# Row numbers by the slot, a halved weight load doubled by ScalarE, and a last group in two pairs

## The chip, the cores and the metric

The kernel runs on one core of a Trainium2 chip. The core has five engines with a queue of instructions each, worked off in order: TensorE (PE; its weight loads are listed as PEld), VectorE (DVE), ScalarE (ACT), GpSimd (POOL) and SyncE (SP). In this kernel SP only issues plain transfers and POOL only issues gathers; both kinds run on the core's 16 DMA engines. The metric is the device time of one execution in microseconds; of several runs the median is given.

## The reference

The input x has 2048 tokens of 576 numbers. Two branches are computed and mixed by a gate per token:

```
g = sigmoid((x * gate_w).sum(-1))
a = irfft2(rfft2(x) * (w_r + 1j * w_i))
q1, q2 = halves of x @ w_q            # 32 heads, 128 numbers each
i1 = argmax(q1 @ k1.T); i2 = argmax(q2 @ k2.T)       # of 64 each
e = i1 * 64 + i2                      # one row of 4096, per token and head
b = sum over heads of  weight * gelu(x . u[e]) * v[e]
out = g * a + (1 - g) * b
```

The weight is a softmax over one candidate. u and v have 4096 rows of 576 numbers each.

## The kernel before

**Tiles.** The tokens are 16 tiles `t` of 128 tokens, one token to a partition. The 32 heads are 8 chunks `c` of 4. u and v lie side by side in one table `uv`, so that one gathered row of 1152 numbers brings both.

**Scores.** For each chunk `build_m` multiplies w_q with the keys, in five pieces of 128 of the 576 input columns (the fifth has 64 columns). `load_wq` brings each piece as 8 x 128 columns; in the fifth the 64 columns stand twice in memory, since the low and the high half of the bits of x are later multiplied with them in one go. A build needs its piece and is a run of 16 records on PE. `scores` then takes two tiles at a time, called a slot: PE makes 2 x 512 scores, DVE takes the maximum of each set of 64 (L419), ACT marks which scores are below it (the flags, L427) and adds offsets (L438), and DVE finds the first position by minima (L443, L447, L448, L450) and joins the two positions (L453). ACT writes the row numbers as integers into `ei` (L454). From L447 on this is done for two slots, that is four tiles, at once.

**Groups.** `group(t, c)` is the work of one tile and one chunk. POOL issues four gathers (L486), one a head; DVE makes four dot products with x (L495, whose sum is read out by a short second instruction), ACT takes gelu (L499), DVE multiplies with the weights (L500). Then either DVE adds the four rows of v, scaled, to the tile's sum `y` (L511 for the first, L513), or, for the tiles that `is_d` names, ACT makes four diagonal matrices (L523) and PE adds the rows up in PSUM; its result is taken over by ACT (L537) or DVE (L539). Tiles 0 to 9 have their groups among the scores of the chunks and after them. Tiles 10 to 15 have theirs at the end, in pairs (10, 11), (12, 13), (14, 15), chunk after chunk, so that the last two groups are those of tiles 14 (by PE) and 15 (by DVE) with chunk 7.

**Spectral branch.** When all scores are done, their memory is given to the Fourier branch: `fold`, `unit`, `invert`. `invert(t)` leaves a tile's share in `ga` (L825, L826). `mix` forms y = y * (1 - g) + ga on DVE (L830) and sends the tile out (L831).

**The order.** Every step is a job of a planner (`Plan.order`) before the program is built. A job has an engine, a duration that the planner assumes, a due time `at`, and the jobs and buffers that it needs. At each moment each engine takes, of the jobs that are ready in the planner's own account, the one that is due first; a due time is no earliest time. The planner assumes for a transfer 0.8 us after its issue, a time by its bytes, behind all the transfers before it, and 0.8 us more; for a gather that time is 1.55 us (L202 to L204, L235, L490), and 1.3 us for a change of ACT's table. The order that comes out is fixed for each engine's queue; on the chip a queue waits in that order for whatever is late. Loads and gathered rows share the 12 buffers `uv`; PSUM has four.

The due times that matter below: a load of wq is due 12 us before its slot; in the last group the dot products and sums are due at the group's time, tile 14's mix 2.4 us after it (9 after its own group, and groups are 6.6 apart), and tile 15's mix 9 us after it.

Of the kernel before, what the change touches and what calls it, by code (L numbers as in the profile page):

```python
# [225 lines left out]
def act(n):  # L226
    return 0.165 + n / 1200
# [8 lines left out]


@with_exitstack
def tile_kernel(ctx, tc, xn, xT, x5, wqT, kT, wri, uv, gw, t_kr, t_fi, t_tw, t_io, out):
    nc = tc.nc  # L240
    PS = bass.MemoryType.PSUM

# [71 lines left out]
    def ld(us, at, fn, w, r=(), **kw):  # L314
        return plan("SP", 0.06, at, lambda: on("SP", fn()), w, r, move=us, **kw)
# [22 lines left out]

    def load_wq(c, i, at, after=()):
        w = wq_t[c, i] = buf("uv", ROW, view=lambda x: x.rearrange("p a d -> p (a d)")[:, : 8 * P].rearrange("p (g e) -> p g e", g=8))  # L340
        ld(load(P * 4096, 4096), at, lambda: nc.sync.dma_start(w.ap, wqT[c, i]), [w], after=after)

    def load_x(b, i, at, at2, n=1):
        st = buf("uv", ROW, view=lambda x: x.rearrange("p a d -> p (a d)")[:, : n * 512])
# [49 lines left out]
    def scores(c, tp, at):  # L394
        if tp == 0:
            mx[c] = buf("mx", [P, NT, 2 * HPC])
        ps = psum()

        def part(j, i):
            t = 2 * tp + j  # L400
            b = t // 4
            tsl = slice((t % 4) * P, (t % 4) * P + P)
            mh, ml = m_t[c, i]
            x = xts[i if i < 4 else 8][b]
            seq = [(x, mh), (x, ml)] + ([(xts[4 + i][b], mh)] if i < 4 else [])

            def go():
                for n, (xx, m) in enumerate(seq):
                    mm(ps.ap[:, j, :], xx.ap[:, tsl], m.ap, start=i == n == 0, stop=i == 4 and n == len(seq) - 1)

            use = {id(q): q for pair in seq for q in pair}
            return plan("PE", 0.23 * len(seq), at, go, [(ps, j)], list(use.values()))

        seq = [(j, i) for i in range(ND) for j in range(2)] if tp in (0, 7) else [(j, i) for j in range(2) for i in range(ND)]
        js = [part(j, i) for j, i in seq]
        score_jobs[c, tp] = js
        mv = mx[c]
        s = c * 8 + tp
        dv(dve(1024, True), at, lambda: nc.vector.tensor_reduce(  # L419
            mv.ap[:, 2 * tp : 2 * tp + 2, :], ps.ap.rearrange("p a (g e) -> p a g e", e=E), AX.X, ALU.max),  # L420
            [(mv, tp)], [(ps, 0), (ps, 1)])
        sg = buf("sg", [P, 2, 2 * HPC, E], BF16)

        def signs(j, g0):
            def go():
                for g in range(g0, g0 + 4):
                    on("ACT", actv(  # L427
                        sg.ap[:, j, g, :], ps.ap[:, j, g * E : g * E + E], AF.Sign,
                        bias=mv.ap[:, 2 * tp + j, g : g + 1], scale=-1.0))
            plan("ACT", 4 * 0.216, at, go, [sg], [(ps, j), (mv, tp)])  # L430

        for j in range(2):
            for g0 in (0, 4):
                signs(j, g0)
        s2 = lambda: sg.ap.rearrange("p a g e -> p (a g) e")
        Q = E // 4
        for b in range(1, 4):
            ac(act(256), at, lambda b=b: actv(s2()[:, :, b * Q : b * Q + Q], s2()[:, :, b * Q : b * Q + Q], AF.Copy, bias=b / 4), [sg], [])  # L438
        if tp % 2 == 0:
            halves[:] = [buf("sq", [P, 2, 4 * HPC, E // 2], BF16)]  # L440
        sq = halves[0]
        k = tp % 2
        dv(0.07 + 512 / 1920, at, lambda: vt(sq.ap[:, k], s2()[:, :, : E // 2], s2()[:, :, E // 2 :], ALU.min), [(sq, k)], [sg])  # L443
        if k == 0:
            return
        q2 = lambda: sq.ap.rearrange("p s g e -> p (s g) e")
        dv(0.07 + 512 / 1920, at, lambda: vt(q2()[:, :, :Q], q2()[:, :, :Q], q2()[:, :, Q:], ALU.min), [sq], [(sq, 0), (sq, 1)])  # L447
        dv(0.07 + 512 / 1920, at, lambda: vt(q2()[:, :, :Q], q2()[:, :, :Q], ramp.ap[:, :Q].unsqueeze(1).to_broadcast([P, 8 * HPC, Q]), ALU.add), [sq], [ramp])  # L448
        im = buf("im", [P, 4, HPC, 2])
        dv(0.06 + 512 / 960, at, lambda: nc.vector.tensor_reduce(  # L450
            im.ap.rearrange("p a h b -> p (a h b)"), q2()[:, :, :Q], AX.X, ALU.min), [im], [sq])
        fe = buf("fe", [P, 4, HPC])
        dv(0.1, at, lambda: stt(fe.ap, im.ap[:, :, :, 0], float(E), im.ap[:, :, :, 1], op0=ALU.mult, op1=ALU.add), [fe], [im])  # L453
        ac(0.18, at, lambda: actv(ei[tp // 2][:, :, 4 * c : 4 * c + 4], fe.ap, AF.Copy, scale=float(E)), [("ei", tp // 2, c)], [fe])  # L454

    def soften(c, t0, t1, at):
        n = t1 - t0
# [18 lines left out]
    accs = {}  # L476
    sums = {}

    def group(t, c, at, ahead, gate_by=()):
        rows = []  # L480
        for k in range(HPC):
            g = buf(("uv", "uv2"), ROW)
            h = c * HPC + k

            def go(g=g, h=h):
                on("POOL", nc.gpsimd.indirect_dma_start(  # L486
                    out=g.ap.rearrange("p a d -> p (a d)"), out_offset=None, in_=uv,
                    in_offset=bass.IndirectOffsetOnAxis(ap=ei[t // 4][:, t % 4, h : h + 1], axis=0)))

            plan("POOL", 1.13, at - ahead, go, [(g, 0), (g, 1)], [("ei", t // 4, c)], move=1.55, after=gate_by)  # L490
            rows.append(g)
        z, b, a = (buf(n, [P, HPC]) for n in ("z", "b", "a"))
        x = xs[t]
        for k in range(HPC):
            dv(0.68, at, lambda k=k, g=rows[k]: stt(  # L495
                g.ap[:, 0, :], g.ap[:, 0, :], 1.0, x.ap, op0=ALU.mult, op1=ALU.mult, accum_out=z.ap[:, k : k + 1]),
                [(z, k), (rows[k], 0)], [x])
        zk = [(z, k) for k in range(HPC)]
        ac(0.18, at - 9, lambda: actv(b.ap, z.ap, AF.Gelu_apprx_tanh), [b], zk, table="gelu")  # L499
        dv(0.08, at, lambda: stt(a.ap, b.ap, 1.0, sw[:, t, c * HPC : c * HPC + HPC], op0=ALU.mult, op1=ALU.mult),  # L500
           [a], [b, ("sw", t, c)])
        new = t not in accs
        if not is_d(t, c):
            if new:
                accs[t] = buf("xn", [P, D])
            y = accs[t]
            for k in range(HPC):
                v = lambda k=k: rows[k].ap[:, 1, :]
                s = lambda k=k: a.ap[:, k : k + 1]
                if new and k == 0:  # L510
                    dv(0.4, at, lambda: nc.vector.tensor_scalar(y.ap, v(0), s(0), None, op0=ALU.mult), [y], [(rows[0], 1), a])  # L511
                else:
                    dv(0.73, at, lambda v=v, s=s: stt(y.ap, v(), s(), y.ap, op0=ALU.mult, op1=ALU.add), [y], [(rows[k], 1), a])  # L513
            return
# [61 lines left out]
    for s in range(NCH * 8):  # L576
# [18 lines left out]
            add_best(c, L0, NT, at + 6, lambda c=c: lc[:, :, c * HPC : c * HPC + HPC], ("lc", c))  # L595
        while todo and todo[0][0] * 8 / NE + LE <= s + 1:
            n, (t, cc) = todo[0]
            if cc * 8 + t // 4 * 2 + 1 > s or (t >= 8 and cc * 8 + 7 > s):
                break
            todo.pop(0)  # L600
            group(t, cc, due(n), AHEAD)
# [226 lines left out]
    def mix(t, at):  # L828
        ga, y = gas[t], accs[t]
        dv(0.73, at, lambda: stt(y.ap, y.ap, gone[:, t : t + 1], ga.ap, op0=ALU.mult, op1=ALU.add), [y], [(ga, 0), (ga, 1), "gone"])  # L830
        ld(load(P * 2304, 2304), at - 5, lambda: nc.sync.dma_start(out[t], y.ap), [], [y])  # L831

    TR = T0 + TLAG
# [9 lines left out]
    for n, t in enumerate(E_T + L_SEQ):  # L843
        at = inv0 + FPACE * 4.2 * n
        invert(t, at)
        if t in E_T:
            mix(t, at + 5)
    for n, (t, c) in enumerate(SEQ):
        group(t, c, TR + TGS * n, AHEAD, score_jobs[NCH - 1, 7][:1])
        if c == NCH - 1:  # L850
            mix(t, TR + TGS * n + 9)
    opened = False
    for j in plan.order():
        if not opened and j.start >= plan.switch:
# [6 lines left out]
        j.fn()  # L861


NT2 = 4
NG = 12
NG2 = 2
# [5 lines left out]
TLAG = 10.0  # L872
FPACE = 1.4
BUILD = (1, 3, 5, 8, 8)
E_T = tuple(range(NE))
L_SEQ = tuple(range(NE, NT))
_PAIRS = [L_SEQ[i : i + 2] for i in range(0, NT - NE, 2)]
# [5 lines left out]
    return t % 2 == 0 if t >= NE else t in (1, 4, 8)  # L883


_INS = ["xn", "xT", "x5", "wqT", "kT", "wri", "uv", "gw", "t_kr", "t_fi", "t_tw", "t_io"]


def _layout(A_x, A_w_r, A_w_i, B_w_q, B_k1, B_k2, B_u, B_v, gate_w):
# [1 line left out]
    x = np.asarray(A_x)[0]  # L891
    xn = c(x.reshape(16, NT, 8, D).transpose(1, 0, 2, 3).reshape(NT, P, D))
    xt = xn.reshape(S, D).T
    w = np.asarray(B_w_q).reshape(D, H * 2, P).transpose(2, 1, 0)
    w = np.concatenate([w, w[:, :, 512:]], 2).reshape(P, NCH, 8, ND, P).transpose(1, 3, 0, 2, 4)
    k1, k2 = np.asarray(B_k1).T, np.asarray(B_k2).T
    wri = np.stack([np.asarray(A_w_r).reshape(P, 16, DF), np.asarray(A_w_i).reshape(P, 16, DF)], 2).transpose(1, 0, 2, 3)
    wri = np.concatenate([wri[:9], wri[9:, ::-1]], 0)
    arrays = {
        "xn": xn, "xT": c(xt[: 4 * P].reshape(4, P, S).transpose(1, 0, 2)), "x5": c(xt[4 * P :]),  # L900
        "wqT": c(w), "kT": c(np.concatenate([k1, k2, k1], 1)), "wri": c(wri),
        "uv": c(np.concatenate([np.asarray(B_u), np.asarray(B_v)], 1)), "gw": c(gate_w),
    }
    arrays.update(_tables())
# [20 lines left out]
```

## Time and profile before

| | |
|---|---|
| median of 3 runs | 975.5 us (974.54 to 977.47) |
| profiled execution | 975.66 us, of it span from first to last instruction 973.9 us |
| granted TensorE clock, mean | 0.981 |
| gathers (POOL) | 512, 302.02 MB |
| all DMA traffic | 346.97 MB, mean 356 GB/s |
| loads of wq | 40 of 512 KB |

A line of a profile names an engine, a line of the kernel, an operation and its tiles as "written<-read" without buffer numbers. L299 stands for all matmuls, since one helper records them. Busy times are sums over the span. A releaser in brackets is what ended an idle time, inferred from semaphores. Scores run from about 10 to 586 us, folds and units to about 850, inverts to the end.

### The profile page before, as it was taken

The page shows a single profiled execution, that of the slowest core. Times are in us where ns is not written, and L with a number is a line of the kernel's source. Part 1 is how long each engine was busy: PE and PEld are TensorE (multiplying, and loading weights), DVE is VectorE, ACT ScalarE, POOL GpSimd, SP SyncE. Part 2 cuts the span into 40 slices and gives each one's busy share as a digit, 9 for nine tenths or more (in the row PEclk, how much of TensorE's full clock was granted, in tenths as well). Part 3 has the DMA queues.
Part 4 walks back from the last instruction along what each step waited for, and adds up shares of the span by engine and source line. Part 5 has one row for each costly group of instructions (what it writes and reads, how often), then busy time and mean ns, then how long its engine had stood idle before and what let it go on. Part 6 is the DMA issues. An engine that isn't in the chain of part 4 may idle for free. (4 is left out here: it accounts for less than half of the span.)

```text
span 973.9 us, 14306 instructions
## 1 busy us (share of the span) xinstructions
PE 909.2 (93%) x4256; PEld 741.6 (76%) x4256; DVE 898.1 (92%) x2119; ACT 511.6 (53%) x1855; POOL 574.7 (59%) x516
## 2 busy tenths in 40 slices
PE   7999999999999999999999994887988898899995
PEld 7887887878888888888888874775677777577774
DVE  3879999999999999999999999999999999987666
ACT  3866686576676586586586674613122122233342
POOL 0056666566666656656657666577666655676650
PEclk9999999999999999999999996999899999999998
DMA  9679999999999999999999999999999999999993
GB/s 323 229 255 362 403 344 335 392 331 379 370 343 382 366 343 369 375 343 360 382 335 380 342 354 392 340 396 409 411 357 411 382 352 371 356 386 392 399 389 110
DMA packets 90893, 346.97 MB, mean 356 GB/s; under 512 B 10240, under 2 KB 10752, under 8 KB 90816
## 3 DMA queue, kind: packets, MB, share of 16 engines
q0 software_dynamic: 73728, 302.02, 81.8%
q1 hardware_dynamic: 17088, 44.03, 12.6%
q8 instruction: 34, 0.56, 0.2%
q14 instruction: 43, 0.35, 0.1%
HBM read 341.30 MB, written 4.72 MB: 355 GB/s over the span
## 5 line engine op out<-in xcount | busy, mean ns | idle before, releaser
L486 POOL DMA_INDIRECT uv<-uv,ei x512 | 574.5, 1122 | 377.3 <-PE p L299 118.2
L299 PE MATMUL p<-mh,xt 128*128 128x512 f32 x1152 | 379.0, 399 | 0.0
L427 ACT ACTIVATE sg<-p,mx 128x64 bf16<-128x64 f32 x1024 | 226.8, 349 | 105.1 <-DVE mx L419 103.1
L299 PEld LDWEIGHTS p<-mh,xt 128*128 128x128 f32 x1152 | 216.9, 188 | 48.7
L299 PE MATMUL p<-ml,xt 128*128 128x512 f32 x640 | 251.8, 393 | 0.0
L513 DVE SCALAR_TENSOR_TENSOR xn<-uv,a,xn 128x576 f32<-128x576 f32 x310 | 250.9, 810 | 1.0
L495 DVE SCALAR_TENSOR_TENSOR uv<-uv,xn 128x576 f32<-128x576 f32 x320 | 235.7, 748 | 11.3 <-DMA uv<-uv,ei 11.2
L299 PE MATMUL p<-uv,dg 128*128 128x288 f32 x768 | 200.6, 416 | 20.3 <-ACT dg L523 15.9
L299 PEld LDWEIGHTS p<-uv,dg 128*128 128x128 f32 x768 | 146.5, 194 | 66.4 <-ACT dg L523 21.0
L299 PEld LDWEIGHTS p<-ml,xt 128*128 128x128 f32 x640 | 120.7, 189 | 26.8
L495 DVE SCALAR_TENSOR_TENSOR uv<-uv,xl 128x576 f32<-128x576 f32 x192 | 140.8, 749 | 0.3 <-DMA uv<-uv,ei 0.2
L499 ACT ACTIVATE b<-z 128x4 f32<-128x4 f32 x128 | 27.1, 211 | 159.6 <-DVE uv L495 158.8
L299 PE MATMUL p<-fi,bt 128*128 128x289 f32 x384 | 101.1, 416 | 9.5 <-DVE t L704 4.4
L299 PEld LDWEIGHTS p<-fi,bt 128*128 128x128 f32 x384 | 84.1, 243 | 24.2 <-issue 8.2
L299 PEld LDWEIGHTS p<-kT,uv 128*128 128x128 f32 x640 | 77.8, 195 | 8.4 <-issue 4.7
L299 PE MATMUL p<-kT,uv 128*128 128x128 f32 x640 | 78.6, 279 | 5.3 <-DMA uv<-wqT 5.2
L419 DVE TENSOR_REDUCE mx<-p 128x16 f32<-128x1024 f32 x64 | 77.7, 1214 | 5.6 <-PE p L299 5.6
L438 ACT ACTIVATE sg<-sg 128x256 bf16<-128x256 bf16 x192 | 74.4, 429 | 1.1
L523 ACT ACTIVATE dg<-ident,a 128x128 f32<-128x128 f32 x192 | 61.4, 393 | 15.2 <-DVE a L500 15.0
L299 PE MATMUL p<-tw,t 128*128 128x256 f32 (+1 forms) x256 | 40.3, 332 | 4.5 <-DVE t L705 2.2
L299 PEld LDWEIGHTS p<-tw,t 128*128 128x128 f32 (+1 forms) x256 | 29.6, 150 | 15.7 <-issue 7.9
L299 PE MATMUL p<-kr,f 128*128 128x128 f32 x160 | 24.3, 316 | 14.4 <-DVE f L646 12.9
(90 smaller groups left out, 642.0 us busy)
## 6 DMA issues: line engine op xcount, KB each, us to landing
uv<-wqT SPq DMA_DIRECT2D x40, 512.0 KB, 6.6
uv<-uv,ei POOLq DMA_INDIRECT x512, 7.0
w<-wri SPq DMA_DIRECT2D x16, 289.0 KB, 6.7
out<-xn SPq DMA_DIRECT2D x16, 288.0 KB, 6.5
xn<-xn SPq DMA_DIRECT2D x10, 288.0 KB, 5.8
tw<-t_tw SPq DMA_DIRECT2D x9, 256.0 KB, 6.5
uv<-xT SPq DMA_DIRECT2D x8, 256.0 KB, 6.7
uv<-xT SPq DMA_DIRECT2D x4, 512.0 KB, 8.4
```

The lines of the kernel that those rows point to most:

```text
L299: after("PE", nc.tensor.matmul(*args, **kw))
L419: dv(dve(1024, True), at, lambda: nc.vector.tensor_reduce(mv.ap[:, 2 * tp : 2 * tp + 2, :], ps.ap.rearrange("p a (g e) -> p a g e", e=E), ...
L427: on("ACT", actv(sg.ap[:, j, g, :], ps.ap[:, j, g * E : g * E + E], AF.Sign, bias=mv.ap[:, 2 * tp + j, g : g + 1], scale=-1.0))
L438: ac(act(256), at, lambda b=b: actv(s2()[:, :, b * Q : b * Q + Q], s2()[:, :, b * Q : b * Q + Q], AF.Copy, bias=b / 4), [sg], [])
L486: on("POOL", nc.gpsimd.indirect_dma_start(out=g.ap.rearrange("p a d -> p (a d)"), out_offset=None, in_=uv, in_offset=bass.IndirectOffsetOn ...
L495: dv(0.68, at, lambda k=k, g=rows[k]: stt(g.ap[:, 0, :], g.ap[:, 0, :], 1.0, x.ap, op0=ALU.mult, op1=ALU.mult, accum_out=z.ap[:, k : k + 1 ...
L499: ac(0.18, at - 9, lambda: actv(b.ap, z.ap, AF.Gelu_apprx_tanh), [b], zk, table="gelu")
L513: dv(0.73, at, lambda v=v, s=s: stt(y.ap, v(), s(), y.ap, op0=ALU.mult, op1=ALU.add), [y], [(rows[k], 1), a])
L523: ac(0.3, at - 9, lambda k=k, dg=dg: actv(dg.ap, ident, AF.Copy, scale=a.ap[:, k : k + 1]), [dg], [a, "ident"])
```

## The change

Three places change, and one input is added.

1. **Row numbers.** For chunk 0 and the first two slots (`EARLY = 2`) the search from L447 on is done after each slot, for its two tiles, instead of after both slots for four. The entries of `ei` are noted by the slot, and `group` waits for its own slot's.
2. **wq.** The fifth piece is stored once (`wq5`, 8 x 64 columns). It is loaded into the second half of its buffer; ACT copies it to the first 64 columns of each of the 8 blocks and then from there to the last 64. The build waits for both copies. The copies are due 2 us after the load's due time.
3. **The end.** `mix` no longer sends; `send` does, with the due time as before. For the last group tile 15's mix comes first (due 4 us before the group), on the sum of its first seven chunks. The group is then made in two parts, heads 0 and 1 at the group's time and heads 2 and 3 due 3.3 us later; each has its own gelu and product, which takes (1 - g) in, and its sums go onto the mixed tile.

```
     def load_wq(c, i, at, after=()):
         w = wq_t[c, i] = buf("uv", ROW, view=...)
-        ld(load(P * 4096, 4096), at, lambda: nc.sync.dma_start(w.ap, wqT[c, i]), [w], after=after)
+        if i < 4:
+            ld(load(P * 4096, 4096), at, lambda: nc.sync.dma_start(w.ap, wqT[c, i]), [w], after=after)
+            return
+        flat = lambda: w.ap.rearrange("p g e -> p (g e)")[:, 512:]
+        ld(load(P * 2048, 2048), at, lambda: nc.sync.dma_start(flat(), wq5[c]), [w], after=after)
+        ac(act(512), at + 2, lambda: actv(w.ap[:, :, :E], flat().rearrange("p (g e) -> p g e", e=E), AF.Copy), [w], [])
+        ac(act(512), at + 2, lambda: actv(w.ap[:, :, E:], w.ap[:, :, :E], AF.Copy), [w], [])
...
-        if k == 0:
+        one = c == 0 and tp < EARLY
+        if k == 0 and not one:
             return
-        q2 = lambda: sq.ap.rearrange("p s g e -> p (s g) e")
+        lo, n = (k, 1) if one else (0, 2)
+        tps = range(tp // 2 * 2 + lo, tp + 1)
+        q2 = lambda: sq.ap[:, lo : lo + n].rearrange("p s g e -> p (s g) e")
...
-    def group(t, c, at, ahead, gate_by=()):
+    def group(t, c, at, ahead, gate_by=(), ks=range(HPC), mixed=False):
...
-            plan("POOL", 1.13, at - ahead, go, [(g, 0), (g, 1)], [("ei", t // 4, c)], move=1.55, after=gate_by)
+            plan("POOL", 1.13, at - ahead, go, [(g, 0), (g, 1)], [("ei", t // 2, c)], move=1.55, after=gate_by)
...
+        part_of = lambda: gone[:, t : t + 1] if mixed else 1.0
...
     def mix(t, at):
         ga, y = gas[t], accs[t]
         dv(0.73, at, lambda: stt(y.ap, y.ap, gone[:, t : t + 1], ga.ap, op0=ALU.mult, op1=ALU.add), [y], [(ga, 0), (ga, 1), "gone"])
+
+    def send(t, at):
+        y = accs[t]
         ld(load(P * 2304, 2304), at - 5, lambda: nc.sync.dma_start(out[t], y.ap), [], [y])
...
     for n, (t, c) in enumerate(SEQ):
-        group(t, c, TR + TGS * n, AHEAD, score_jobs[NCH - 1, 7][:1])
+        at = TR + TGS * n
+        if n == len(SEQ) - 1:
+            mix(t, at - 4)
+            for ks in LAST:
+                group(t, c, at + 1.65 * ks[0], AHEAD, held, ks, True)
+        else:
+            group(t, c, at, AHEAD, held)
+            if c == NCH - 1:
+                mix(t, at + 9)
         if c == NCH - 1:
-            mix(t, TR + TGS * n + 9)
+            send(t, at + 9)
...
+EARLY = 2
+LAST = (0, 1), (2, 3)
```

More of the change, by code (lines that the diff above doesn't have):

```diff
@@ L238, in tile_kernel @@
 @with_exitstack
-def tile_kernel(ctx, tc, xn, xT, x5, wqT, kT, wri, uv, gw, t_kr, t_fi, t_tw, t_io, out):
+def tile_kernel(ctx, tc, xn, xT, x5, wqT, wq5, kT, wri, uv, gw, t_kr, t_fi, t_tw, t_io, out):
     nc = tc.nc
@@ L443, in scores @@
         dv(0.07 + 512 / 1920, at, lambda: vt(sq.ap[:, k], s2()[:, :, : E // 2], s2()[:, :, E // 2 :], ALU.min), [(sq, k)], [sg])
-        if k == 0:
+        one = c == 0 and tp < EARLY
+        if k == 0 and not one:
             return
-        q2 = lambda: sq.ap.rearrange("p s g e -> p (s g) e")
-        dv(0.07 + 512 / 1920, at, lambda: vt(q2()[:, :, :Q], q2()[:, :, :Q], q2()[:, :, Q:], ALU.min), [sq], [(sq, 0), (sq, 1)])
-        dv(0.07 + 512 / 1920, at, lambda: vt(q2()[:, :, :Q], q2()[:, :, :Q], ramp.ap[:, :Q].unsqueeze(1).to_broadcast([P, 8 * HPC, Q]), ALU.add), [sq], [ramp])
+        lo, n = (k, 1) if one else (0, 2)
+        tps = range(tp // 2 * 2 + lo, tp + 1)
+        q2 = lambda: sq.ap[:, lo : lo + n].rearrange("p s g e -> p (s g) e")
+        keys = [(sq, x) for x in range(lo, lo + n)]
+        dv(0.07 + n * 256 / 1920, at, lambda: vt(q2()[:, :, :Q], q2()[:, :, :Q], q2()[:, :, Q:], ALU.min), keys, [])
+        dv(0.07 + n * 256 / 1920, at, lambda: vt(q2()[:, :, :Q], q2()[:, :, :Q], ramp.ap[:, :Q].unsqueeze(1).to_broadcast([P, n * 4 * HPC, Q]), ALU.add), keys, [ramp])
         im = buf("im", [P, 4, HPC, 2])
-        dv(0.06 + 512 / 960, at, lambda: nc.vector.tensor_reduce(
-            im.ap.rearrange("p a h b -> p (a h b)"), q2()[:, :, :Q], AX.X, ALU.min), [im], [sq])
+        dv(0.06 + n * 256 / 960, at, lambda: nc.vector.tensor_reduce(
+            im.ap[:, : 2 * n].rearrange("p a h b -> p (a h b)"), q2()[:, :, :Q], AX.X, ALU.min), [im], keys)
         fe = buf("fe", [P, 4, HPC])
-        dv(0.1, at, lambda: stt(fe.ap, im.ap[:, :, :, 0], float(E), im.ap[:, :, :, 1], op0=ALU.mult, op1=ALU.add), [fe], [im])
-        ac(0.18, at, lambda: actv(ei[tp // 2][:, :, 4 * c : 4 * c + 4], fe.ap, AF.Copy, scale=float(E)), [("ei", tp // 2, c)], [fe])
+        dv(0.1, at, lambda: stt(fe.ap[:, : 2 * n], im.ap[:, : 2 * n, :, 0], float(E), im.ap[:, : 2 * n, :, 1], op0=ALU.mult, op1=ALU.add), [fe], [im])
+        ac(0.18, at, lambda: actv(ei[tp // 2][:, 2 * lo : 2 * lo + 2 * n, 4 * c : 4 * c + 4], fe.ap[:, : 2 * n], AF.Copy, scale=float(E)),
+           [("ei", x, c) for x in tps], [fe])
     def soften(c, t0, t1, at):
@@ L477, in tile_kernel @@
     sums = {}
-    def group(t, c, at, ahead, gate_by=()):
-        rows = []
-        for k in range(HPC):
+    def group(t, c, at, ahead, gate_by=(), ks=range(HPC), mixed=False):
+        rows = {}
+        for k in ks:
             g = buf(("uv", "uv2"), ROW)
@@ L488, in go @@
                     in_offset=bass.IndirectOffsetOnAxis(ap=ei[t // 4][:, t % 4, h : h + 1], axis=0)))
-            plan("POOL", 1.13, at - ahead, go, [(g, 0), (g, 1)], [("ei", t // 4, c)], move=1.55, after=gate_by)
-            rows.append(g)
+            plan("POOL", 1.13, at - ahead, go, [(g, 0), (g, 1)], [("ei", t // 2, c)], move=1.55, after=gate_by)
+            rows[k] = g
         z, b, a = (buf(n, [P, HPC]) for n in ("z", "b", "a"))
         x = xs[t]
-        for k in range(HPC):
+        k0, k1 = ks[0], ks[-1] + 1
+        for k in ks:
             dv(0.68, at, lambda k=k, g=rows[k]: stt(
@@ L497, in group @@
                 [(z, k), (rows[k], 0)], [x])
[L498 to L501, printed above, removed]
+        zk = [(z, k) for k in ks]
+        ac(0.18, at - 9, lambda: actv(b.ap[:, k0:k1], z.ap[:, k0:k1], AF.Gelu_apprx_tanh), [b], zk, table="gelu")
+        part_of = lambda: gone[:, t : t + 1] if mixed else 1.0
+        dv(0.08, at, lambda: stt(a.ap[:, k0:k1], b.ap[:, k0:k1], part_of(), sw[:, t, c * HPC + k0 : c * HPC + k1], op0=ALU.mult, op1=ALU.mult),
+           [a], [b, ("sw", t, c)] + ["gone"] * mixed)
         new = t not in accs
@@ L506, in group @@
             y = accs[t]
-            for k in range(HPC):
+            for k in ks:
                 v = lambda k=k: rows[k].ap[:, 1, :]
@@ L597, in tile_kernel @@
             n, (t, cc) = todo[0]
-            if cc * 8 + t // 4 * 2 + 1 > s or (t >= 8 and cc * 8 + 7 > s):
+            if cc * 8 + (t // 2 if cc == 0 and t // 2 < EARLY else t // 4 * 2 + 1) > s or (t >= 8 and cc * 8 + 7 > s):
                 break
@@ L847, in tile_kernel @@
             mix(t, at + 5)
+            send(t, at + 5)
+    held = score_jobs[NCH - 1, 7][:1]
     for n, (t, c) in enumerate(SEQ):
-        group(t, c, TR + TGS * n, AHEAD, score_jobs[NCH - 1, 7][:1])
+        at = TR + TGS * n
[7 more added lines that the diff above has]
+                mix(t, at + 9)
         if c == NCH - 1:
-            mix(t, TR + TGS * n + 9)
+            send(t, at + 9)
     opened = False
@@ L883, in is_d @@
     return t % 2 == 0 if t >= NE else t in (1, 4, 8)
-_INS = ["xn", "xT", "x5", "wqT", "kT", "wri", "uv", "gw", "t_kr", "t_fi", "t_tw", "t_io"]
+_INS = ["xn", "xT", "x5", "wqT", "wq5", "kT", "wri", "uv", "gw", "t_kr", "t_fi", "t_tw", "t_io"]
 def _layout(A_x, A_w_r, A_w_i, B_w_q, B_k1, B_k2, B_u, B_v, gate_w):
@@ L893, in _layout @@
     xt = xn.reshape(S, D).T
-    w = np.asarray(B_w_q).reshape(D, H * 2, P).transpose(2, 1, 0)
-    w = np.concatenate([w, w[:, :, 512:]], 2).reshape(P, NCH, 8, ND, P).transpose(1, 3, 0, 2, 4)
+    w = np.asarray(B_w_q).reshape(D, NCH, 8, P).transpose(1, 3, 2, 0)
     k1, k2 = np.asarray(B_k1).T, np.asarray(B_k2).T
@@ L900, in _layout @@
         "xn": xn, "xT": c(xt[: 4 * P].reshape(4, P, S).transpose(1, 0, 2)), "x5": c(xt[4 * P :]),
-        "wqT": c(w), "kT": c(np.concatenate([k1, k2, k1], 1)), "wri": c(wri),
+        "wqT": c(w[..., : 4 * P].reshape(NCH, P, 8, 4, P).transpose(0, 3, 1, 2, 4)), "wq5": c(w[..., 4 * P :].reshape(NCH, P, 512)), "kT": c(np.concatenate([k1, k2, k1], 1)), "wri": c(wri),
         "uv": c(np.concatenate([np.asarray(B_u), np.asarray(B_v)], 1)), "gw": c(gate_w),
```

## The prediction

> **What bounds the kernel now.** I read the busy times first, then the windows by stage, then the chain of waits, then the timelines where the three edits act. In a window row the columns are window, length, and busy time (with instructions) of PE, PEld, DVE, ACT, POOL, then the granted clock, the DMA share and GB/s.
>
> ```profile
> span 973.9 us, 14306 instructions
> ...
> PE 909.2 (93%) x4256; PEld 741.6 (76%) x4256; DVE 898.1 (92%) x2119; ACT 511.6 (53%) x1855; POOL 574.7 (59%) x516
> ```
>
> ```profile
> 48.00:72.00 24.00, 24.00 (x130) 20.48 (x129) 17.47 (x42) 16.93 (x69) 12.89 (x12) 1.00 0.69 249
> 96.00:500.00 404.00, 401.19 (x1941) 332.34 (x1942) 396.60 (x927) 275.37 (x1060) 250.06 (x222) 1.00 0.96 362
> 500.00:600.00 100.00, 87.75 (x394) 71.95 (x393) 99.90 (x234) 67.58 (x262) 68.81 (x61) 0.94 0.98 362
> 620.00:852.00 232.00, 201.81 (x894) 159.41 (x893) 225.72 (x549) 57.43 (x184) 151.96 (x140) 0.97 0.99 381
> 852.00:950.00 98.00, 97.43 (x401) 75.87 (x401) 72.93 (x173) 34.80 (x90) 64.84 (x58) 1.00 1.01 391
> ```
>
> ```profile
> 852.62 104.51 PE p L299 x428
> ```
>
> From 96 to 852 us DVE is hardly ever idle; PE is as full until about 500 and then has gaps. So DVE time carries the middle: what DVE gains early stays gained, as long as it never runs dry, and what it loses there is lost. From 852.62 the chain is one run of 428 matmuls, whose start is set by the DVE work before it. DVE idles in two places that the change touches: 6.5 us of the window from 48 to 72 (24.00 - 17.47), and a gap at the very end.
>
> **Row numbers per slot.** The first gather waits for the row numbers of tiles 0 to 3 together (columns from here: start, duration, engine, line, operation, tiles, and in brackets the idle time before it and what ended that).
>
> ```profile
> 34.38 0.42 DVE L443 TENSOR_TENSOR sq<-sg 128x512 bf16<-128x512 bf16 x1
> 49.26 0.68 DVE L450 TENSOR_REDUCE im<-sq 128x32 f32<-128x512 bf16 x1
> 51.19 0.22 ACT L454 ACTIVATE ei<-fe 128x16 uint32<-128x16 f32 x1 [1.67 <-DVE fe L453]
> 51.68 1.08 POOL L486 DMA_INDIRECT uv<-uv,ei  x1 [51.23 <-DVE sq L443]
> 52.63 1.23 DVE L419 TENSOR_REDUCE mx<-p 128x16 f32<-128x1024 f32 x1 [1.14 <-PE p L299]
> 56.44 0.76 DVE L495 SCALAR_TENSOR_TENSOR uv<-uv,xn 128x576 f32<-128x576 f32 x1 [2.15 <-DMA uv<-uv,ei]
> 59.13 0.76 DVE L495 SCALAR_TENSOR_TENSOR uv<-uv,xn 128x576 f32<-128x576 f32 x1 [1.93 <-DMA uv<-uv,ei]
> 60.62 1.28 ACT L499 ACT_TABLE_LOAD   x1
> 60.96 0.76 DVE L495 SCALAR_TENSOR_TENSOR uv<-uv,xn 128x576 f32<-128x576 f32 x1 [1.06 <-DMA uv<-uv,ei]
> ```
>
> L443 has taken the flags of slot 0 by 34.8, but the rest of the search waits for slot 1. After the change it follows at once: four short DVE steps and one ACT step, about 2 us, so row numbers near 37 and first dot products, 4.8 us behind their gather as now (51.68 to 56.44), near 42. The eight gathers of tiles 0 and 1 are then in before DVE first goes idle. The four idle pieces above (1.14 + 2.15 + 1.93 + 1.06) are 6.3 us, and the dot products and sums of two tiles, over eight steps of 0.7 us, are enough to fill them. The gathers have room: the DMA share is 0.69 in this stretch against 0.96 later. They take eight of the twelve `uv` buffers some 15 us sooner, which the SP queue's loads of wq share; those are issued well ahead of use, so I count nothing, and if that cover fails a load comes late by about one landing, 6.5 us by a row below, shared by PE.
>
> The added DVE work is one more set of the four steps after L443, on half the elements. If time goes with size it is nothing; if each costs like L450, four times 0.68 is 2.7. I take 0.3, since these are short steps with most of their time in the elements. Gain: 6.3 - 0.3 = 6.0. Bounds: 6.5 gained (all of the window's idle time), and, with no idle time filled, 2.7 lost.
>
> Earlier dot products also call for an earlier gelu. It lands between two exponentials, so ACT may switch tables twice more, 2 x 1.28 = 2.6 us in a stretch where it has little idle time. The planner charges 1.3 for a switch when it sets the order, so DVE is given other work meanwhile and I add nothing; uncovered, it is 2.6 us once. Beside that row: the Trainium skill, "ScalarE: Activation LUTs", section "What ACT_TABLE_LOAD costs", states about 2.66 us per switch, a drain of 1.38 included, by which the two would be an estimated 5.3. A table load at 278.07 (below) is followed by its ACTIVATE at 279.36, so no drain stands behind it here.
>
> **The halved load and ScalarE's two copies.** Eight loads shrink from 512 to 256 KB, and sixteen copies of 512 elements a partition come onto ACT.
>
> ```profile
> L352 ACT ACTIVATE xt<-uv x20: 629/671/743, 5.8 to 38.2; 128x512 fp32r<-128x512 f32 x16, 64x512 fp32r<-64x512 f32 x4
> L341 SPq DMA_DIRECT2D uv<-wqT x2: 578/594/611, 5.3 to 5.9; - x2
> DMA to landing us min/median/max: 8.7/9.1/9.5
> 14.81 3.77 PEld L299 LDWEIGHTS p<-kT,uv 128*128 128x128 f32 x32
> L341 SPq DMA_DIRECT2D uv<-wqT x27: 327/328/408, 129.4 to 493.8; - x27
> DMA to landing us min/median/max: 3.6/6.5/10.6
> L341 SPq DMA_DIRECT2D uv<-wqT x2: 327/328/328, 275.7 to 276.2; - x2
> DMA to landing us min/median/max: 6.7/7.3/8.0
> 278.07 1.28 ACT L471 ACT_TABLE_LOAD   x1
> 279.36 0.22 ACT L471 ACTIVATE cand<-cand 128x24 f32<-128x24 f32 x1
> 280.44 1.03 ACT L438 ACTIVATE sg<-sg 128x256 bf16<-128x256 bf16 x3
> 283.29 0.42 DVE L443 TENSOR_TENSOR sq<-sg 128x512 bf16<-128x512 bf16 x1
> 284.07 0.20 ACT L499 ACTIVATE b<-z 128x4 f32<-128x4 f32 x1
> 285.36 0.15 DVE L500 SCALAR_TENSOR_TENSOR a<-b,sw 128x4 f32<-128x4 f32 x1
> 289.36 3.73 PE L299 MATMUL p<-kT,uv 128*128 128x128 f32 x32
> ```
>
> L352 is the nearest copy: 16 x 0.671 = 10.7 us of ACT, which is busy only 275 of 404 us in the long stretch. As work it is free. At the start the load issued at 5.9 lands by 15.4, and PE comes to it halfway through its 32-piece run, near 16.7; the half load lands up to 0.7 sooner (256 KB at 362 GB/s), and two copies of 0.67 behind it end between 16.1 and 16.8. Bounds there: 0.7 gained, 1.3 lost; I take 0. Later PE is covered too: of the pair issued at 275.7 and 276.2 the slower lands at 284.2, while its build starts about 291.
>
> What is not covered is the order. The queues are in order, and the planner sets a copy's place by its own figure for the landing: on an empty queue 0.06 + 0.8 + 0.85 + 0.8 = 2.5 us after the issue (L202 to L204, with the transfer by L235). The trace's median is 6.5. Now PE has 5 us and more in hand for this load; the copies give the wait to ACT, and behind it in ACT's queue stand the flags and gelus that DVE takes soon after: 1.82 us at L443 (281.47 to 283.29), 1.09 at L500 (284.27 to 285.36). The planner's figure grows by 1.55 for every gather that it has queued, and with a gather each 1.8 us (404 / 222) it mostly has one or two queued. So ACT reaches the copies 4.0 - 3.1 = 0.9 to 4.0 - 1.55 = 2.45 us early, on average 1.7; less the 1.09 in hand that is 0.6 to 0.7 of DVE at each of the six later boundaries (the second chunk's loads go out early): **4 us lost**. Ends: 0, and 2.45 x 6 = 14.7 with nothing in hand.
>
> The bytes saved, 2.1 MB, are 5.8 us of DMA at 362 GB/s, spread over 500 us in which DVE hardly waits for a gather; I count 0, and at most those 5.8 are gained.
>
> **The last group.** The first row is the last gather.
>
> ```profile
> L486 POOL DMA_INDIRECT uv<-uv,ei x1: 1043/1043/1043, 951.3 to 951.3; - x1
> DMA to landing us min/median/max: 5.7/5.7/5.7
> 959.39 0.75 DVE L495 SCALAR_TENSOR_TENSOR uv<-uv,xl 128x576 f32<-128x576 f32 x1
> 960.51 0.49 ACT L826 ACTIVATE xl<-p,gsc 128x287 f32<-128x287 f32 x1
> 964.68 0.82 DVE L830 SCALAR_TENSOR_TENSOR xn<-xn,gone,xl 128x576 f32<-128x576 f32 x1 [4.53 <-ACT xn L537]
> 965.41 0.75 DVE L495 SCALAR_TENSOR_TENSOR uv<-uv,xl 128x576 f32<-128x576 f32 x1
> 966.64 3.38 DVE L513 SCALAR_TENSOR_TENSOR xn<-uv,a,xn 128x576 f32<-128x576 f32 x4
> 970.06 0.82 DVE L830 SCALAR_TENSOR_TENSOR xn<-xn,gone,xl 128x576 f32<-128x576 f32 x1
> ```
>
> DVE stands 4.53 us before tile 14's mix while the fourth dot product of the last group, whose row landed at 957.0, is queued behind it. After it come gelu, four sums and tile 15's mix, to 970.88; 3.0 us later the output is out. The change moves tile 15's mix and the first two sums ahead. The mix needs L826, done at 961.00; mix, gelu and two sums then fit roughly into the hole. The second pair is due later (+3.3) than tile 14's mix (+2.4), so at least its last dot product stays behind the mix. Then: mix to 965.4, dot product, 1.23 us from its start to the first sum as now, two sums of 0.83: 968.3. If one sum slips behind as well, 969.1; if the whole pair's dot products do, 969.0. I take 968.7: **2.2 us gained**. Bounds: 4.8 if all of it ends before the mix, and 0 if the last gather comes late. No loss, since three steps leave the end of the chain and the one more gelu and product lie inside these figures. POOL's order is as before (the two gathers due later were its last two), and the store keeps its place on SP.
>
> **Sum.** -6.0 + 4.0 - 2.2 = -4.2 us. The profiled execution took 975.66 (span 973.9 and 1.8 around it), 0.2 above the median: 971.4.
>
> **The rivals.** *The copies never wait* (chance 0.22): the planner has two or more gathers queued at each boundary and the slack covers the rest. 975.5 - 8.2 = 967.3. For it: the 3.6 us that the fastest of 27 loads took; against it: the median. [...]
>
> *ACT's wait goes through to DVE* (0.18), the slower one: at each boundary one gather is queued in the planner's figure and nothing is in hand, 14.7 us. 975.5 - 8.2 + 14.7 = 982. It decides from 8.2 / 6 = 1.4 us a boundary, and the kernel is slower than 0.3% from 1.85. For it: slack under 2 us in both places shown; against it: ACT's idle third.
>
> *DVE's head start is lost* (0.15): PE, full until 500, sets when the scores end, and DVE runs dry waiting for them. Then 975.5 + 0.3 + 4 - 2.2 = 977.6. For it: 401 of 404 us PE; against it: DVE's 99.90 of 100 from 500 to 600, where PE is the one that waits.
>
> **How the numbers follow.** My case has 0.45, with some 3 us either way (968 to 975). 0.3%, about what a measurement of this kernel can tell from no change, is 2.9 us. Faster: the first rival's 0.22 and three quarters of 0.45, 0.56. Same: the rest of 0.45 and most of the third, 0.24. Slower: 0.20. The range, 965 to 980.5, reaches past 967.3 and takes the near half of the slower rival.
>
> **What would show it.** Right: the first gather near 37 to 40; DVE busy over 22 us from 48 to 72; ACT waiting for "DMA uv<-wq5" in total under 15 us and DVE for L438 or L499 under 6; a last mix of tile 14 followed by two sums. Wrong: PE waiting in the first 100 us, loads of wq5 that hold ACT longer than 3 us at a boundary, a run of matmuls that starts no earlier than 852, or an order at the end with three or more sums behind tile 14's mix.

## The result and the profile after

| | before | after |
|---|---|---|
| median | 976.18 us (973.17 to 978.22, 18 runs) | 981.46 us (976.85 to 984.73, 18 runs) |
| profiled execution, span | 975.66, 973.9 us | 983.57, 981.8 us |
| ratio to before, 95% interval | 1 | 1.0056 (1.0042 to 1.007) |

The kernel is slower by 0.56%, 5.5 us; 971.4 was predicted, and 981.46 lies above the range's end of 980.5. The profiled execution after is 2.1 us above its median. All ratios leave out executions that ran slower as a whole; most of these, four of twelve and one of them 2381 us long, were of the kernel called "all, chunk 1 by the slot" below.

The windows of the kernel after, with the columns of those of before:

```profile
48.00:72.00 24.00, 24.00 (x115) 19.79 (x114) 22.50 (x61) 22.49 (x80) 11.29 (x11) 1.00 0.89 315
96.00:500.00 404.00, 393.72 (x1891) 325.38 (x1890) 381.85 (x889) 265.54 (x1018) 240.50 (x213) 0.99 0.93 342
96.00:200.00 104.00, 99.15 (x464) 81.32 (x463) 92.01 (x214) 65.03 (x250) 55.27 (x51) 0.97 0.88 324
200.00:400.00 200.00, 195.31 (x951) 161.92 (x950) 191.57 (x448) 133.10 (x513) 122.74 (x109) 1.00 0.95 347
500.00:600.00 100.00, 96.02 (x431) 77.63 (x430) 97.97 (x230) 71.63 (x278) 63.87 (x59) 1.00 0.96 346
620.00:852.00 232.00, 204.90 (x921) 164.51 (x920) 226.91 (x556) 63.35 (x205) 149.55 (x138) 0.96 0.99 382
```

From 48 to 72 us DVE does what was forecast: 22.50 us in place of 17.47. Then it loses more than that: from 96 to 600 its busy time falls from 396.60 + 99.90 = 496.50 to 381.85 + 97.97 = 479.82, by 16.7 us. Some 7.1 us of this go between 96 and 200 and as much between 200 and 400, where these were the rows before:

```profile
96.00:200.00 104.00, 102.08 (x494) 84.22 (x495) 99.13 (x235) 69.07 (x270) 63.89 (x57) 1.00 0.95 362
200.00:400.00 200.00, 199.12 (x963) 165.11 (x962) 198.69 (x465) 136.74 (x520) 126.78 (x113) 1.00 0.97 366
```

After 620 it is no worse than before. PE's last matmul of the scores ends at 597.2 in place of 584.1, and the run of matmuls that carries the end starts 9.9 us later than at 852.62:

```profile
862.50 104.51 PE p L299 x428
```

What DVE waits for from 96 to 600 us, first before, then after (engine, line, what it waited for: us in total, times, longest):

```profile
DVE uv L495 <- DMA uv<-uv,ei: 5.6, 10, 1.0
DVE mx L419 <- PE p L299: 0.8, 3, 0.4
DVE sw L472 <- ACT cand L471: 0.4, 1, 0.4
```

```profile
DVE uv L507 <- DMA uv<-uv,ei: 16.3, 20, 2.2
DVE xn L552 <- PE p L299: 3.3, 2, 3.0
DVE a L513 <- ACT b L511: 1.9, 2, 1.6
DVE uv L507 <- PE p L299: 1.6, 1, 1.6
DVE mx L425 <- PE p L299: 0.4, 2, 0.2
```

L507 is the dot product that was L495. The five rows after sum to 23.5 us, the three before to 6.8: the difference is the lost 16.7. By far the largest part, 10.7, is dot products that DVE reaches before their gathered row is there. PE shows what fits the same lateness passed on: in the order of a group, a late dot product makes a late gelu, then a late diagonal matrix (L536, before L523). PE's waits for these matrices from 96 to 600 us, before and after:

```profile
PE p L299 <- ACT dg L523: 1.3, 1, 1.3
PE p L299 <- ACT dg L536: 11.4, 9, 3.1
```

One such place, in the timelines of POOL and DVE after (start, duration, engine, line, operation, tiles, idle time before it). The chain of work that ended last goes through this very pair:

```profile
296.04 1.18 POOL L497 DMA_INDIRECT uv<-uv,ei  x1 [0.30 <-DVE a L513]
```

```profile
300.30 0.41 DVE L449 TENSOR_TENSOR sq<-sg 128x512 bf16<-128x512 bf16 x1
301.62 0.76 DVE L507 SCALAR_TENSOR_TENSOR uv<-uv,xn 128x576 f32<-128x576 f32 x1 [0.91 <-DMA uv<-uv,ei]
```

The gather is issued at 296.04 and DVE is ready for its row 4.7 us later, at 300.71 (301.62 - 0.91). It starts on the row 5.6 us after the issue, which is still less than the median. The medians from issue to landing on the page after (KB each, us):

```profile
uv<-uv,ei POOLq DMA_INDIRECT x512, 7.2
...
uv<-wq SPq DMA_DIRECT2D x8, 256.0 KB, 8.6
```

The planner, which places the dot product, assumes 1.13 + 0.8 + 1.55 + 0.8 = 4.3 us for a gather with no transfer queued ahead of it. The kernel before lived with that figure because its order, as it came out, mostly left more room.

There is a second visible change. POOL's timeline about 121 us, before and after:

```profile
121.96 0.94 POOL L486 DMA_INDIRECT uv<-uv,ei  x1 [2.70 <-ACT ei L454]
```

```profile
37.45 3.44 POOL L497 DMA_INDIRECT uv<-uv,ei  x1 [37.00 <-DMA uv<-wqT]
...
121.69 1.03 POOL L497 DMA_INDIRECT uv<-uv,ei  x1 [10.33 <-ACT ei L464]
```

Gathers start 14 us earlier than before (37.45 against 51.68), but by 121 us both kernels have issued the same 40 gathers, all that chunk 0 has for tiles 0 to 9, and wait for the row numbers of chunk 1. These come when PE has made chunk 1's scores, at the same moment in both. So POOL waits 10.33 us where it waited 2.70. Theory H came from this: the head start runs dry there. Theory R came after the first four runs below: the order made for parts 1 and 2 together takes dot products too soon behind their gathers.

### The profile page after: what moved, and what is told of

It reads as the page before. It is cut to its first block, busy times and chain, and to the rows that moved or that the text cites. A ratio compares the mean times of both kernels' runs of the same rounds, so it can differ in the third digit from the quotient of the medians.

```text
span 981.8 us, 14354 instructions
## 1 busy us (share of the span) xinstructions
PE 912.6 (93%) x4256; PEld 744.4 (76%) x4256; DVE 899.2 (92%) x2124; ACT 520.3 (53%) x1875; POOL 572.8 (58%) x516
## 2 busy tenths in 40 slices
DMA packets 90893, 344.87 MB, mean 351 GB/s; under 512 B 10240, under 2 KB 10752, under 8 KB 90816
## 4 chain that ended last, share of the span: by engine, by line
DVE 38%; PE 38%; DMA 10%; issue 8%; POOL 3%; ACT 2%; POOLq 0%; SPq 0%; ACTq 0%; DVEq 0%
PE p L299 38%; DVE uv L507 13%; DVE xn L526 11%; DMA uv<-uv,ei 9%; POOL uv L497 3%; DVE mx L425 3%; DVE im L460 1%; ACT sg L433 1%; DMA uv<-wq 1%; DVE ml L394 1%; DVE sq L449 1%; DVE xn L552 1%; DVE bt L782 1%; DVE t L716 1%; DVE a L513 1%
## 5 line engine op out<-in xcount | busy, mean ns | idle before, releaser
L507 DVE SCALAR_TENSOR_TENSOR uv<-uv,xn 128x576 f32<-128x576 f32 x320 | 235.0, 749 | 20.8 <-DMA uv<-uv,ei 19.1
L299 PE MATMUL p<-uv,dg 128*128 128x288 f32 x768 | 204.7, 422 | 27.3 <-ACT dg L536 25.2
L299 PEld LDWEIGHTS p<-uv,dg 128*128 128x128 f32 x768 | 148.9, 197 | 75.0 <-ACT dg L536 32.8
L507 DVE SCALAR_TENSOR_TENSOR uv<-uv,xl 128x576 f32<-128x576 f32 x192 | 141.1, 750 | 0.6 <-DMA uv<-uv,ei 0.5
L299 PEld LDWEIGHTS p<-kT,uv 128*128 128x128 f32 x640 | 79.9, 198 | 8.0 <-issue 5.0
L536 ACT ACTIVATE dg<-ident,a 128x128 f32<-128x128 f32 x192 | 62.1, 395 | 12.5 <-DVE a L513 12.2
```

The source lines that it names most:

```text
L299: after("PE", nc.tensor.matmul(*args, **kw))
L507: dv(0.68, at, lambda k=k, g=rows[k]: stt(g.ap[:, 0, :], g.ap[:, 0, :], 1.0, x.ap, op0=ALU.mult, op1=ALU.mult, accum_out=z.ap[:, k : k + 1 ...
L536: ac(0.3, at - 9, lambda k=k, dg=dg: actv(dg.ap, ident, AF.Copy, scale=a.ap[:, k : k + 1]), [dg], [a, "ident"])
```

## The experiments

In the diffs "-" is the changed kernel unless said otherwise. Part 1 is the row numbers by the slot, part 2 the halved load with its copies, part 3 the end. Ratios are to the kernel before, run beside each on the same chip. The pairs and the two mended kernels ran on a chip where the kernel before itself took 991.4 us, against 976 to 978 on the others, so across chips only ratios are compared.

**One part at a time.** At this stage the theories were H and W, that ScalarE's waits for the halved load go through to DVE. Part 1 alone takes the diffs of parts 2 and 3 back:

```
-        if i < 4:
-            ld(load(P * 4096, 4096), at, lambda: nc.sync.dma_start(w.ap, wqT[c, i]), [w], after=after)
-            return
...
+        ld(load(P * 4096, 4096), at, lambda: nc.sync.dma_start(w.ap, wqT[c, i]), [w], after=after)
...
-            mix(t, at - 4)
-            for ks in LAST:
-                group(t, c, at + 1.65 * ks[0], AHEAD, held, ks, True)
...
+        group(t, c, TR + TGS * n, AHEAD, score_jobs[NCH - 1, 7][:1])
...
+            mix(t, TR + TGS * n + 9)
```

> Part 1 alone (row numbers by the slot in chunk 0; wq and the end as before). Theory H, head start runs dry: the gathers reach the end of chunk 0 sooner, then wait about 10 us at 110 to 122 us for the row numbers of chunk 1, with no rows in hand, and the DVE idles more from 96 to 600: 4 to 8 us slower than before (980 to 984). Theory W, ScalarE waits for the halved load: this part keeps its head start, 4 to 6 us faster (970 to 972). My prediction: 6.0 faster.

Measured: 977.08 us, 1.001 (0.9991 to 1.0029). The windows of part 1 alone:

```profile
48.00:72.00 24.00, 24.00 (x118) 19.93 (x117) 23.66 (x60) 21.27 (x79) 10.83 (x11) 1.00 0.86 320
72.00:96.00 24.00, 21.93 (x102) 17.54 (x101) 18.76 (x46) 12.63 (x51) 15.65 (x15) 0.93 0.92 326
```

DVE gains 6.2 us from 48 to 72 and gives 4.6 back in the next 24, where it was busy 23.40 before. What it waits for in these 24 us (L501 is the dot product here):

```profile
DVE uv L501 <- DMA uv<-uv,ei: 4.2, 3, 1.7
DVE uv L501 <- PE p L299: 1.0, 1, 1.0
```

POOL then waits 9.77 us for chunk 1's row numbers, until 123.88, and DVE gives back another 3.3 us between 96 and 200. So the head start is lost, but more than half of it to gathered rows that are late before H's place is reached, and the kernel is not slower for it: the wait that H names is there, H's price of 4 to 8 us is not.

Part 2 alone takes back part 3 as above, and part 1 by its constant:

```
-EARLY = 2
+EARLY = 0
```

> Part 2 alone (halved fifth piece, two ScalarE copies; rows and end as before). Theory W: 8 to 15 us slower (984 to 991) with ScalarE idle before L346 for more than 10 us in all. Theory H: within 3 us of before, ScalarE idle before the copies under 3 us in all. My prediction: 4 us slower.

Measured: 975.57 us, 0.9985 (0.9968 to 1.0003). ScalarE waited 0.6 us in all for the halved loads, in two places. W falls, and with it the 4 us forecast.

Part 3 alone takes back part 2 as above and part 1 by the constant:

> Part 3 alone (last group in two pairs on a mixed tile). Both theories: 2.2 us faster (973 to 975), all of it after 950 us; the trace before 930 us as before.

Measured: 973.58 us, 0.9967 (0.9949 to 0.9984): 3 us faster, a little more than both theories had.

Parts 2 and 3, with only the constant changed:

> Parts 2 and 3, without part 1. Theory H: about 2 us faster than before (973 to 976), the loss of the whole change gone. Theory W: 6 to 13 us slower (982 to 989).

Measured: 974.73 us, 0.9976 (0.996 to 0.9992). So every part alone is harmless or good. Their sum, 1.0 - 1.5 - 3.2 = -3.7 us by the ratios, is not what the whole change shows, +5.5.

**The parts in pairs.** Parts 1 and 2, with part 3 taken back as above:

> Parts 1 and 2 of the change, the end as before. Part 1 alone was 1.001 of before, part 2 alone 0.9985, the end alone 0.9967. Theory R (together the two parts give an order in which DVE takes dot products too soon behind the issue of their gathers; the order of the changed kernel has 11 of them less than 6 us behind, part 1 alone has 2 and part 2 alone none): the loss of the whole change comes back here without the end's gain, 983 to 986 us, ratio 1.007 to 1.011, and DVE waits 12 us or more for gathered rows between 96 and 600 us. Rival S (the parts simply add, and the changed kernel's 1.0056 comes from the end's part in this company): 0.9995 of before, 974 to 978 us, DVE's waits for gathered rows under 10 us.

Measured: 1.0109 (1.0065 to 1.0154). The loss is there without part 3, 0.0114 above the 0.9995 to which the two parts add, with 15.0 us of DVE waiting for gathers. The rival S, by which the parts simply add, falls.

Parts 1 and 3, with part 2 taken back as above:

> Parts 1 and 3, wq loaded as before. Theory R (the loss needs parts 1 and 2 together): the parts add, 1.001 - 0.0033 = 0.998 of before, 973 to 976 us, DVE's waits for gathered rows between 96 and 600 us near part 1's 8.6. Rival S (the loss comes from part 1 and the end together): 980 us or more.

Measured: 0.9976 (0.9945 to 1.0007), as the parts add; DVE waits 9.8 us for gathers. The loss comes with parts 1 and 2 together.

**Mending the order, or the row numbers.** The first kernel changes one figure of the planner and nothing of the work. The second makes the row numbers of chunk 1's first two slots by the slot as well. In the first, 4.3 us for a gather become 6.3:

```
-                    got.end = dma + 0.8
+                    got.end = dma + (0.8 + 2.0 * (eng == "POOL"))
```

> The changed kernel, with the planner's landing of a gather 2 us later (6.3 us behind the issue in place of 4.3; the trace's median is 7.2). The order is made anew; no dot product stands less than 6 us behind its gather's issue in it, where the changed kernel has 11. Theory R: DVE's waits for gathered rows between 96 and 600 us fall from 16.3 to 6 us or less, and the time to 970 to 976 us. Theory H (the loss is the row numbers of chunk 1 that come when PE has made their scores, and DVE running dry behind them): POOL still waits some 10 us near 121, and the time stays at 979 to 983.

Measured: 0.9936 (0.9914 to 0.9959), faster than before. DVE's waits from 96 to 600 us in this kernel:

```profile
DVE uv L507 <- DMA uv<-uv,ei: 4.4, 7, 0.9
```

POOL's wait for chunk 1's row numbers is still there in its timeline:

```profile
118.06 0.94 POOL L497 DMA_INDIRECT uv<-uv,ei  x1 [8.74 <-ACT ei L464]
```

So 1.2% went with the waits for gathers, and the wait that H named stayed. The second kernel:

```
-        one = c == 0 and tp < EARLY
+        one = c in CH and tp < EARLY
...
-            if cc * 8 + (t // 2 if cc == 0 and t // 2 < EARLY else t // 4 * 2 + 1) > s or (t >= 8 and cc * 8 + 7 > s):
+            if cc * 8 + (t // 2 if cc in CH and t // 2 < EARLY else t // 4 * 2 + 1) > s or (t >= 8 and cc * 8 + 7 > s):
...
+CH = (0, 1)
```

> The changed kernel, with the row numbers by slot for the first two slots of chunk 1 too, so that the gathers of chunk 1 need not wait for its second slot. Theory H: POOL's wait of 10.3 us that ends at 121.7 shrinks to 5 or less, DVE gains about 3 us between 96 and 200, and the time falls to 972 to 977. Theory R: the head start is no cause of the 300 to 400 us loss; unless the new order happens to have fewer short leads, 979 to 983 us, with DVE still waiting over 12 us for gathered rows.

Measured: 1.0043 (1.0014 to 1.0072). The wait at 121 is gone: POOL issues gathers from 113.75 to 130 with at most 1.69 us of idle time between them.

```profile
96.00:200.00 104.00, 99.25 (x474) 81.32 (x473) 97.14 (x231) 69.21 (x265) 56.51 (x52) 1.00 0.90 330
200.00:400.00 200.00, 191.63 (x927) 158.23 (x926) 185.91 (x431) 128.71 (x493) 118.19 (x106) 0.99 0.93 343
```

DVE is busy 97.14 us from 96 to 200, where the changed kernel has 92.01, but 185.91 from 200 to 400, where that has 191.57, and it waits 16.1 us for gathers from 96 to 600. The gain comes early and is lost later, as R has it.

**The same figure on the kernel before.** If leads that are too short are the cause, they must slow a kernel that has none of the three parts. "-" is the kernel before:

```
-                    got.end = dma + 0.8
+                    got.end = dma + (0.8 + -2.0 * (eng == "POOL"))
```

> The kernel before, with none of the three parts; the planner's landing of a gather is 2 us sooner (2.3 us behind the issue in place of 4.3). The order made so has 9 dot products less than 6 us behind their gather's issue and 29 less than 7, where the kernel before has 0 and 8, and the changed kernel 11 and 24. Theory R (such dot products are what the changed kernel lost its time to): DVE waits 12 us or more for gathered rows between 96 and 600 us (before 5.6), and the time is 0.5 to 1.1% longer, ratio 1.005 to 1.011. Rival L (the loss belongs to the parts themselves, and short leads are a mark of it, not its cause): 0.998 to 1.002.

Measured: 993.18 us, 1.0142 (1.0112 to 1.0172), more than expected. From 96 to 600 us DVE waits 14.5 us for gathers, 18 times. Over the whole span, the kernel before first and this one behind it:

```profile
DVE uv L495 <- DMA uv<-uv,ei: 11.4, 15, 2.2
```

```profile
DVE uv L495 <- DMA uv<-uv,ei: 24.9, 28, 2.5
```

The waits grow by 13.5 us and the time by 13.9 (0.0142 of 977.55). That they agree so closely is in part chance: from 96 to 600 DVE's idle time grows by 12.0 us, 8.9 of them waits for gathers. The granted clock of TensorE was lower too, 0.974 to 0.978 in these runs against 0.978 to 0.983 in the kernel before beside them; as an estimate, if all the time went with that clock, this is 0.6%, less than half of the loss, and whether it is a cause or comes of the waits was not tested. Rival L, no loss at all, falls. The control goes the other way:

```
-                    got.end = dma + 0.8
+                    got.end = dma + (0.8 + 2.0 * (eng == "POOL"))
```

> The kernel before, with the planner's landing of a gather 2 us later. Control for the run later_landing, which took the changed kernel from 1.0056 to 0.9936 of before. Theory R: the order before has no dot product less than 6 us behind its gather and 5.6 us of such waits in all, so at most these can go: 0.995 to 1.000. Rival L' (a later landing helps any order by as much, so that it says nothing of the changed kernel): 0.990 or less.

Measured: 978.35 us, 1.0008 (0.9992 to 1.0023), just past R's 1.000, with waits of 7.7 us that did not shrink. Rival L' falls too: the later landing mends the changed kernel, and the kernel before has nothing to mend.

**Versions that beat both.** Parts 1 and 3 with the later landing, part 2 taken back; and the whole change with the later landing and the row numbers by the slot in chunks 0 and 1 (the diffs above together):

> Parts 1 and 3 with wq loaded as before, and the landing of a gather 2 us later for the planner. Without the later landing this was 0.9976 of before, with 9.8 us of DVE's waits for gathered rows. Theory R: the waits fall to 5 us or less, the time by 2 to 5 us: 0.992 to 0.996. If later_landing's gain needs part 2 (fewer bytes beside the gathers), 0.997 or more.

Measured: 970.75 us, 0.9931 (0.9906 to 0.9956). The time is as expected; DVE's waits for gathers, 7.0 us, are above the 5 that R had.

> The changed kernel with both: row numbers by slot for the first two slots of chunk 1 too, and the landing of a gather 2 us later for the planner. later_landing was 0.9936 with an 8.7 us wait of POOL for chunk 1's row numbers at 118. If that wait still costs DVE time (about 4 us of the 6.9 that it idles between 96 and 200), 0.989 to 0.992; if it is covered by the rows in hand, 0.993 to 0.996.

Measured: 969.91 us, 0.9923 (0.9901 to 0.9945), waits 5.2 us; this lies between the two cases expected and decides for neither. The three kernels with the later landing, 0.9936, 0.9931 and 0.9923, can't be told apart; neither part 2 nor the row numbers of chunk 1 show a gain of their own there.

All kernels, by DVE's waits for gathered rows from 96 to 600 us, in traces from several chips. The last column counts, in the order as the planner wrote it and for the same 504 us of its own account, the dot products that stand less than 6 us behind their gather's issue:

| kernel | ratio | DVE waits for gathers, us | so close behind, in the order |
|---|---|---|---|
| part 2 | 0.9985 | 3.5 | 0 |
| parts 2 and 3 | 0.9976 | 4.1 | 0 |
| all, later landing | 0.9936 | 4.4 | 0 |
| all, later landing, chunk 1 by the slot | 0.9923 | 5.2 | 0 |
| before | 1 | 5.6 | 0 |
| parts 1 and 3, later landing | 0.9931 | 7.0 | 0 |
| before, later landing | 1.0008 | 7.7 | 0 |
| part 1 | 1.001 | 8.6 | 2 |
| part 3 | 0.9967 | 9.2 | 0 |
| parts 1 and 3 | 0.9976 | 9.8 | 2 |
| before, sooner landing | 1.0142 | 14.5 | 9 |
| parts 1 and 2 | 1.0109 | 15.0 | 11 |
| all, chunk 1 by the slot | 1.0043 | 16.1 | 11 |
| after (all) | 1.0056 | 16.3 | 11 |

Two groups stand apart: up to 9.8 us none is slower than 1.001, from 14.5 all are slower by 0.4% or more. Inside a group the waits do not rank the kernels. The rows are also fewer than they look: part 3 leaves the planner's order up to 600 us exactly as it was, so that rows which differ by part 3 alone show one order twice, and their waits differ by up to 3.6 us (5.6 and 9.2).

What is shown is that the order costs the time: the same work in an order made with a later landing loses the waits and the loss, and the kernel before, in an order made with a sooner landing, gets both. The experiments moved the whole order, not the close pairs alone, and these are a mark of it more than the whole price. If the dot products of the changed kernel's trace are matched one by one with the planner's order, 5 of the 11 close pairs wait, 6.2 us together; another 9.3 us stand at pairs that the planner put 6 to 8 us behind. Of the 16.3 us, 4.6 come between 127 and 149 us, right behind the wait of POOL that H names. So H's place has a share of the loss in this order; with the later landing (in a trace from a slower chip), though POOL waits nearly as long, DVE is busy only 2.0 us less than before between 96 and 200, where it lost 7.1. Why parts 1 and 2 together bring such an order out, and neither alone, was not followed job by job.

## Why the prediction was wrong, point by point

- **"What DVE gains early stays gained, as long as it never runs dry."** The condition failed. DVE did run dry, 23.5 us of waits from 96 to 600 against 6.8.
- **Row numbers, -6.0.** The mechanism came: first gather at 37.45 (near 37), first dot product at 45.23 (near 42 was forecast), DVE busy 22.50 us from 48 to 72 (over 22), 5.0 more than before. The added search cost 0.6 us in place of 0.3, and ACT loaded its tables twice more, 36 times against 34. But part 1 alone measured 1.001 in place of 0.994. With part 3 beside it and gathers landing later in the plan the pair is at 0.9931, against 0.9967 for part 3 alone: some 3.5 us for part 1, a difference of two kernels on different chips and so only an estimate. The 6.0 was too much, and it was to be had only in an order that gives the gathers their time.
- **The halved load, +4.0.** Wrong, and on the other side. The step that failed is "ACT reaches the copies 4.0 - 3.1 = 0.9 to 4.0 - 1.55 = 2.45 us early". In the trace after, the first copies of the eight loads start between 7.8 and 17.9 us behind their load's issue (6.19 to 15.46, 505.71 to 514.87), and ScalarE waited 1.6 us in all, at two boundaries, although the median landing is 8.6, above the 6.5 reckoned with. For this part the first rival, copies that hardly wait, was right: they were covered by their place in the order, not by a short transfer.
- **The last group, -2.2.** Right, the mechanism too. The run of matmuls starts 9.9 us later and the profiled execution ends 7.9 later, a gain of 2.0; alone it measured -3.2 us (-5.0 to -1.6 by its interval). The end's order is the one forecast: tile 15's mix (the first L843 row), two sums, then tile 14's mix with two sums behind it. (The upper bound of 4.8 is not worked out there; with all else ahead of the mix, which ran from 964.68 to 965.50 before, it would be 5.4. Nothing rests on it.)

```profile
970.92 0.82 DVE L843 SCALAR_TENSOR_TENSOR xn<-xn,gone,xl 128x576 f32<-128x576 f32 x1 [2.25 <-ACT xl L839]
...
975.08 0.81 DVE L843 SCALAR_TENSOR_TENSOR xn<-xn,gone,xl 128x576 f32<-128x576 f32 x1
...
977.10 1.67 DVE L526 SCALAR_TENSOR_TENSOR xn<-uv,a,xn 128x576 f32<-128x576 f32 x2
```

- **The sum.** The parts measured one by one give -3.7, close to the -4.2 forecast, by cancelling errors. The step that made the prediction wrong is the term put at nothing, "500 us in which DVE hardly waits for a gather; I count 0": it was carried over to the changed kernel without a reason. That cover was taken as given; it belonged to the old order, and in the new one DVE waits 16.3 us for gathers where it waited 5.6. The planner's figure of 2.5 us for a load of wq was set against a measured 6.5, but the same comparison was not made for a gather, 4.3 against 7.0, on which 512 dot products stand.
- **The rivals.** "DVE's head start is lost" happened in part: in part 1 alone the gain is gone, but DVE waits for gathered rows (8.6 us from 96 to 600) and hardly for PE (0.8). That its 977.6 is near part 1's 977.08 says nothing, since that sum holds the terms of the other two parts; for part 1 it gives +0.3, and +1.0 was measured, not told apart. As the main cause of the whole loss the experiments take it out: the loss stays when POOL's wait goes (1.0043) and goes when the wait stays (0.9936). "ACT's wait goes through to DVE" gave 982, near the measured time by luck, for its mechanism did not happen. The one that did, a new order with gathers too close, was not among the rivals.

## What to carry to other kernels

Where a planner writes the queues' order from assumed latencies, an edit anywhere makes a new order everywhere: cost not only the work moved, but compare each assumed latency with the trace's, and ask which waits the old order avoided by luck. Here, with a figure of 4.3 us against a measured 7.2, three parts that are harmless alone became a loss of 0.56%; with 6.3 in its place the same change was a gain of 0.64%. When parts measured alone do not add up to the whole, look at the pairs and at what the new order waits for before blaming a part.

## What the runs showed that was not expected

A load of half the size did not land sooner beside the stream of gathers: 8.6 us is the median for the 256 KB of `wq5` (7.5 in part 2 alone), against 7.5 for the 512 KB loads of the same kernel and 6.6 for those before. The 2.1 MB saved over the run, 344.87 against 346.97 MB, bought no time that the runs can tell (0.9936 with it, 0.9931 without).
